# A decode kernel's last microseconds: the sum of its branches built transposed and stored from 112 partitions, one product per denominator, and the last values in three loads

## The chip, the cores and the metric

The kernel runs on one core of a Trainium2 chip. The metric is the device time of one execution in microseconds (us). Before the change it is 194.76 us (median of four runs, 194.66 to 194.98; of the first three runs, 194.69). Ratios are the mean time of one kernel's fast runs over that of the other's fast runs of the same rounds, with a 95% interval, so they are not quite the ratio of the medians quoted. "Span" is the profile's time from the first to the last instruction, some 1.8 us shorter than the device time. "Landed" is the moment at which the profile shows a transfer reported as complete. SBUF is the core's on-chip memory, which the loads fill; PSUM is where TensorE's sums build up; HBM is the chip's main memory. "Eviction" is the copy of a sum from PSUM to SBUF.

## The reference, cut to what matters

```python
# B=2 rows, D=448, 16 heads on 8 key/value heads, Dh=256, the last W=4096 of 32768 positions
xn = layernorm(x)
q  = xn @ wq
p  = softmax(q @ k_window.T * Dh**-0.5)          # k, v windows: 2*8*4096*256 bf16 each
A  = (p @ v_window) @ wo
Bo = mish(xn @ w1 + b1) @ w2
return x + A + Bo                                 # [2, 1, 448] bf16, 1792 bytes
```

77.66 MB are read for a result of 1792 bytes.

## The kernel before

All large loads go through one queue in program order (x and a bias, 5.3 KB, go through another). For each of 16 pairs of key/value head and row, K is transposed on VectorE, TensorE makes scores, ScalarE the exponentials and their sums, VectorE transposes p, TensorE multiplies with V. The last pair's values come in two loads, then wo in two.

```python
    NO = 2; DO = D // NO
    psA = [ps_a.tile([Bsz, DO], FP32, name=f"psA{n}") for n in range(NO)]
    def add(n, lhsT, rhs, **flags):
        nc.tensor.matmul(psA[n][:, :], lhsT=lhsT, rhs=rhs, skip_group_check=True, **flags)
    # ... x, then act @ w2, then per key/value head:
    def mix(kvh):                                # oT: 128 x (2 rows); w: wo, 128 x 448 per piece
        for h in range(rep):
            for n in range(NO):
                for c in range(ND):
                    add(n, oT[:, c, h, :], w[:, h, c * D + n * DO : c * D + (n + 1) * DO], ...)
    # ... per head: denominators straight from ScalarE's row sums rs
        for n in range(NH):
            nc.tensor.matmul(den[:], lhsT=rs[:, n : n + 1].to_broadcast([P, P]), rhs=hsel[:], ...)
    # ... end
    res = consts.tile([Bsz, D], BF16)            # the last tile of the constants: 896 B in each SBUF partition (row)
    nc.vector.tensor_copy(out=res[:, 0:DO], in_=psA[0][:, :])
    nc.scalar.copy(out=res[:, DO:D], in_=psA[1][:, :])
    nc.sync.dma_start(out=out.flatten_outer_dims(), in_=res[:])
```

The pools of the load tiles (wo, k, v) lie in SBUF behind the constants, in this order.

The softmax here doesn't subtract the row's maximum and nothing guards it: scores larger than these inputs give would overflow.

Of the kernel before, what the change touches and what calls it, by code (L numbers as in the profile page):

```python
# [9 lines left out]
ALU = mybir.AluOpType  # L10
AXIS = mybir.AxisListType
BF16 = mybir.dt.bfloat16
FP32 = mybir.dt.float32
# [21 lines left out]
def kernel(  # L35
# [13 lines left out]
    nc = tc.nc  # L49
    P = 128  # L50
# [3 lines left out]
    Bsz, Sq, D = A_x.shape  # L54
    _, Hkv, Sk, Dh = A_k_cache.shape
    HqDh = A_wq.shape[1]
    Hq = HqDh // Dh
    rep = Hq // Hkv
# [3 lines left out]
    T = W // P  # L62
    NH = 2
    TH = T // NH
    NX = 2
    NS = D * NX // P
    HW = HqDh // NX
    HF = F // NX
    HH = Hq // NX
    NF = HF // P  # L70
    ND = Dh // P
    NB = Dh // (2 * Q)
    NE = 2
    assert Sq == 1 and D * NX == NS * P and NS % 2 == 1 and HF % P == 0 and Hq % NX == 0
    assert TH * Q <= 512 and NB * NE * Q == Dh and ND == 2
    scale = float(Dh) ** -0.5

    consts = ctx.enter_context(tc.tile_pool(name="consts", bufs=1))
# [5 lines left out]
    small = ctx.enter_context(tc.tile_pool(name="small", bufs=3))  # L84
# [3 lines left out]
    ps_a = ctx.enter_context(tc.tile_pool(name="ps_a", bufs=1, space=PSUM))  # L88
# [3 lines left out]
    x_bf = consts.tile([Bsz, D], BF16)  # L92
# [5 lines left out]
    def v_tile(n):  # L98
        t = v_pool.tile([P, T * Dh], BF16, tag="v", name="v")
        return t[:, 0:n]  # L100
# [6 lines left out]
    for lo, hi in ((0, SC), (SC, NS)):  # L107
        w = v_tile((hi - lo) * HW).rearrange("p (s n) -> p s n", n=HW)
# [4 lines left out]
    ident = consts.tile([P, P], BF16)  # L113
# [11 lines left out]
        out=rstd[:], in_=mv[:, 1:2], func=ACT.Sqrt, bias=eps_t[:], scale=1.0  # L125
# [5 lines left out]
    for r in range(2):  # L131
        n = (NS + 1 - r) // 2
        nc.vector.tensor_scalar(  # L133
            out=xn_bf[:, r : NS : 2, :, :],
            in0=bass.AP(
                x_all.tensor,
                x_all.offset,
                [list(x_all.ap[0]), [1, n], [NS, P // 2], [(NS + r) // 2, 2]],
            ),
            scalar1=mv[:, 0:1],  # L140
            scalar2=rstd[:],
            op0=ALU.subtract,
            op1=ALU.mult,
# [3 lines left out]
    for b4 in range(NB):  # L147
        rows = slice(b4 * Q, (b4 + 1) * Q)
        for j in range(NQ):
            nc.vector.tensor_copy(  # L150
                out=spread[rows, b4, j * Q : (j + 1) * Q], in_=ident[rows, rows]
            )
    hsel = consts.tile([P, rep], FP32)
    nc.vector.tensor_copy(out=hsel[:], in_=ident[:, 0:rep])
    for j in range(1, NQ):
        nc.vector.tensor_tensor(
            out=hsel[:], in0=hsel[:], in1=ident[:, j * Q : j * Q + rep], op=ALU.add
        )
    NW = 3
    qdiag = []  # L160
    for i in range(NW):
        t = consts.tile([P, NB * NE, P], BF16, name=f"qdiag{i}")
# [5 lines left out]
    for s in range(NS):  # L168
# [7 lines left out]
        out=odd[:],  # L176
        in_=ident[:].rearrange("p (u o) -> p o u", o=2),
# [4 lines left out]
    for par in range(2):  # L182
        for x in range(NX):
            which = (par + x) % 2
            nc.vector.tensor_scalar(
                out=xs[:, par : NS : 2, x, :],
                in0=xnT_ps[:, par : NS : 2, :],
                scalar1=odd[:, which : which + 1],
                scalar2=None,
                op0=ALU.mult,  # L190
# [2 lines left out]
    nc.vector.memset(ones[:], 1.0)  # L193


    NO = 2
    DO = D // NO
    psA = [ps_a.tile([Bsz, DO], FP32, name=f"psA{n}") for n in range(NO)]

    def add(n, lhsT, rhs, **flags):  # L200
        nc.tensor.matmul(psA[n][:, :], lhsT=lhsT, rhs=rhs, skip_group_check=True, **flags)  # L201

    for n in range(NO):
        add(n, ident[0:Bsz, 0:Bsz], x_bf[:, n * DO : (n + 1) * DO], start=True, stop=False)


    qrep = consts.tile([P, NB, HH, NE, NX, Bsz], BF16)
# [28 lines left out]
    def build_q(i):  # L236
        kvh, b = heads[i]
        x, h0 = divmod(kvh * rep, HH)
        t = qdiag[i % NW]
        tv = t[:].rearrange("p (n e) c -> p n e c", e=NE)  # L240
# [9 lines left out]
    act_bf = consts.tile([P, NF, NX, Bsz], BF16)  # L250
# [53 lines left out]
    def dense_out():  # L304
        w2_sb = dense.pop("w2")
        for x in range(NX):
            for c in range(NF):
                for n in range(NO):
                    add(
                        n,  # L310
                        act_bf[:, c, x, :],
                        w2_sb[:, x, c, n * DO : (n + 1) * DO],
                        start=False,
                        stop=False,
                    )


    NSTEP = len(heads) * NH
# [3 lines left out]
    def load_k(i):  # L322
        kvh, b = heads[i]
        t = k_pool.tile([P, T * Dh], BF16, tag="k", name="k")
        nc.sync.dma_start(  # L325
            out=t[:], in_=A_k_cache[b, kvh, s0:Sk, :].rearrange("(p t) d -> p (t d)", p=P)
        )
        k_t[i] = t

    def load_v(i, parts=1):  # L330
        kvh, b = heads[i]
        t = v_tile(T * Dh).rearrange("p (t d) -> p t d", t=T)
        vin = A_v_cache[b, kvh, s0:Sk, :].rearrange("(p t) d -> p t d", p=P)
        for u in range(parts):
            ts = slice(u * T // parts, (u + 1) * T // parts)
            nc.sync.dma_start(out=t[:, ts, :], in_=vin[:, ts, :])  # L336
        v_t[i] = t

    def load_wo(kvh, parts=1):
        w = wo_pool.tile([P, rep, ND * D], BF16, tag="wo", name="wo")  # L340
        r0 = kvh * rep * Dh
        win = A_wo[r0 : r0 + rep * Dh, :].rearrange("(h p c) d -> p h (c d)", h=rep, p=P)
        for u in range(parts):
            hs = slice(u * rep // parts, (u + 1) * rep // parts)
            nc.sync.dma_start(out=w[:, hs, :], in_=win[:, hs, :])
        wo_t[kvh] = w

    def turn(s):
        kt = kt_pool.tile([P, TH * Dh], BF16, tag="kt", name="kt")
        i, half = divmod(s, NH)  # L350
        k = k_t[i] if half < NH - 1 else k_t.pop(i)
        nc.vector.transpose(  # L352
            out=kt[:].bitcast(FP32),
            in_=k[:, half * TH * Dh : (half + 1) * TH * Dh].bitcast(FP32),
        )
        kt_t[s] = kt

    def scores(s):
# [3 lines left out]
        for n in range(NB):  # L362
            for e in range(NE):
                nc.tensor.matmul(  # L364
                    psc[:],
                    lhsT=qdiag[i % NW][:, n * NE + e, :],
                    rhs=ktv[:, n, e, :, :],
# [15 lines left out]
    def turn_p(s):  # L383
        pT = p_pool.tile([P, TH * Q], BF16, tag="pT", name="pT", bufs=7)
        nc.vector.transpose(out=pT[:], in_=p_t.pop(s)[:])  # L385
        pT_t[s] = pT
        i, half = divmod(s, NH)
        if half != NH - 1:
            return
        rs = state.pop(("rs", i))  # L390
        den = ps_den.tile([P, rep], FP32, tag="den", name="den")
        for n in range(NH):
            nc.tensor.matmul(  # L393
                den[:],
                lhsT=rs[:, n : n + 1].to_broadcast([P, P]),
                rhs=hsel[:],
                start=(n == 0),
                stop=(n == NH - 1),
            )
        state["rec", i] = small.tile([P, rep], FP32, tag="rec", name="rec", bufs=4)  # L400
        nc.vector.reciprocal(out=state["rec", i][:], in_=den[:])  # L401

# [26 lines left out]
    def mix(kvh):  # L429
        oT = state["oT"]  # L430
        w = wo_t.pop(kvh)
        for h in range(rep):
            for n in range(NO):
                for c in range(ND):
                    add(
                        n,
                        oT[:, c, h, :],
                        w[:, h, c * D + n * DO : c * D + (n + 1) * DO],
                        start=False,
                        stop=(kvh == Hkv - 1 and h == rep - 1 and c == ND - 1),  # L440
                    )

    NK = len(heads)
    KA = 2
# [8 lines left out]
    for i in range(NK + KA):  # L453
        if i + 2 < NK:
            load_k(i + 2)
        if i < NK:
            load_v(i, parts=1 if i < NK - 1 else 2)
            kvh, b = heads[i]
            if b == Bsz - 1:
                load_wo(kvh, parts=1 if i < NK - 1 else 2)  # L460
            for half in range(NH):
                s = i * NH + half
                if s + 1 < NSTEP:
                    turn(s + 1)
                scores(s)
                if s >= 1:
                    turn_p(s - 1)
            if i + 2 < NK:
                build_q(i + 2)
        if i == NK:  # L470
            turn_p(NSTEP - 1)
        if i == 0:
            dense_in()
        if i == 1:
            dense_out()
        if i >= KA:
            values(i - KA)
            kvh, b = heads[i - KA]
            if b == Bsz - 1:
                mix(kvh)  # L480

    res = consts.tile([Bsz, D], BF16)
    nc.vector.tensor_copy(out=res[:, 0:DO], in_=psA[0][:, :])
    nc.scalar.copy(out=res[:, DO:D], in_=psA[1][:, :])  # L484
    nc.sync.dma_start(out=out.flatten_outer_dims(), in_=res[:])
    issue_in_order(tc)


# [28 lines left out]
```

## Time and profile before

| what | before |
|---|---|
| device time, median | 194.76 us |
| span of the profiled run | 192.7 us |
| last values landed | 187.21 us |
| store issued | 190.58 us |
| bytes loaded | 77.66 MB |

The load queue is the bound: the DMA row of the 40 slices is at nine tenths from the second slice to the 38th. What follows the last landing takes 5.5 us. The prediction below shows the lines.

```profile
SPq L512 <- DMA out_dram<-res: 0.7, 1, 0.7
```

### The profile page before, as it was taken

The page shows a single profiled execution, that of the slowest core. Times are in us where ns is not written, and L with a number is a line of the kernel's source. Part 1 is how long each engine was busy: PE and PEld are TensorE (multiplying, and loading weights), DVE is VectorE, ACT ScalarE, POOL GpSimd, SP SyncE. Part 2 cuts the span into 40 slices and gives each one's busy share as a digit, 9 for nine tenths or more (in the row PEclk, how much of TensorE's full clock was granted, in tenths as well). Part 3 has the DMA queues.
Part 4 walks back from the last instruction along what each step waited for, and adds up shares of the span by engine and source line. Part 5 has one row for each costly group of instructions (what it writes and reads, how often), then busy time and mean ns, then how long its engine had stood idle before and what let it go on. Part 6 is the DMA issues. An engine that isn't in the chain of part 4 may idle for free.

```text
span 192.7 us, 3810 instructions
## 1 busy us (share of the span) xinstructions
PE 130.4 (68%) x1624; PEld 81.3 (42%) x1624; DVE 102.2 (53%) x137; ACT 25.5 (13%) x69; POOL 24.8 (13%) x138
## 2 busy tenths in 40 slices
PE   0242993999827985499709881797449592898854
PEld 0142381466513654246504651364324452364752
DVE  4605506996638390929264753838091744748101
ACT  5000110112200211012200220021101110021100
POOL 7004320022110112002200210020200200000000
PEclk9999996699995799669975998599957979589965
DMA  6999999999999999999999999999999999999960
GB/s 211 424 447 408 427 427 435 428 435 402 431 422 428 425 415 428 435 418 414 429 425 432 420 416 430 428 425 411 428 432 428 403 434 422 432 414 429 410 253 2
DMA packets 7674, 77.90 MB, mean 404 GB/s; under 512 B 741, under 2 KB 2793, under 8 KB 3050
## 3 DMA queue, kind: packets, MB, share of 16 engines
q1 hardware_dynamic: 7652, 77.66, 96.1%
q8 instruction: 12, 0.20, 0.4%
q14 instruction: 4, 0.03, 0.0%
q10 hardware_dynamic: 6, 0.01, 0.0%
HBM read 77.67 MB, written 0.00 MB: 403 GB/s over the span
## 4 chain that ended last, share of the span: by engine, by line
DMA 96%; PE 1%; SPq 1%; issue 0%; ACT 0%; DVE 0%
DMA v<-in_A_v_cache_dram 51%; DMA k<-in_A_k_cache_dram 18%; DMA wo<-in_A_wo_dram 17%; DMA v<-in_B_w_dram 10%; PE psA L201 1%; PE o L411 1%; SPq L109 0%; SPq L325 0%; ACT res L484 0%; DVE oT L422 0%; SPq L336 0%
## 5 line engine op out<-in xcount | busy, mean ns | idle before, releaser
L352 DVE STREAM_TRANSPOSE kt<-k 128x2048 f32<-128x2048 f32 x32 | 73.5, 2300 | 48.9 <-DMA k<-in_A_k_cache_dram 48.9
L364 PE MATMUL sc<-kt,qdiag 128*128 128x512 bf16 x256 | 75.0, 443 | 14.4 <-DVE kt L352 14.3
L364 PEld LDWEIGHTS <-qdiag 128*128 128x128 bf16 x256 | 26.1, 111 | 50.5 <-issue 24.1
L374 ACT ACTIVATE p<-sc 128x512 bf16<-128x512 f32 x32 | 19.1, 597 | 144.8 <-PE sc L364 140.9
L244 POOL COPY qdiag<-qrep 32x8 bf16<-32x8 bf16 x128 | 21.0, 186 | 125.3 <-PE sc L364 109.8
L201 PE MATMUL psA<-wo,oT 128*2 128x224 bf16 x64 | 12.5, 370 | 31.3 <-DVE oT L422 31.3
L411 PEld LDWEIGHTS <-v 128*128 128x128 bf16 x1024 | 27.9, 97 | 6.3 <-DMA v<-in_A_v_cache_dram 3.0
L411 PE MATMUL o<-pT,v 128*128 128x2 bf16 x1024 | 28.1, 163 | 2.7 <-DMA v<-in_A_v_cache_dram 2.7
L385 DVE STREAM_TRANSPOSE pT<-p 128x512 bf16<-128x512 bf16 x32 | 21.4, 671 | 0.0
L201 PEld LDWEIGHTS <-oT 128*2 128x2 bf16 x64 | 6.5, 111 | 34.6 <-DVE oT L422 32.0
L393 PEld LDWEIGHTS den<-hsel,rs 128*128 128x128 f32 x64 | 11.7, 227 | 3.8 <-issue 2.1
L401 DVE RECIPROCAL rec<-den 128x2 f32<-128x2 f32 x16 | 2.5, 153 | 18.7 <-PE den L393 18.7
L393 PE MATMUL den<-hsel,rs 128*128 128x2 f32 x64 | 9.4, 252 | 0.0
L215 PE MATMUL qT_ps<-xs,v 128*128 128x4 bf16 x112 | 3.3, 166 | 6.1 <-DMA v<-in_A_wq_dram 6.1
L422 DVE TENSOR_TENSOR oT<-o,rec 128x4 bf16<-128x4 f32 x16 | 2.1, 134 | 8.5 <-PE o L411 8.5
L374 ACT ACTIVATION_READ_ACCUMULATOR p<-sc 128x1 f32 x32 | 6.2, 194 | 0.0
L215 PEld LDWEIGHTS <-v 128*128 128x128 bf16 x112 | 3.1, 104 | 6.6 <-DMA v<-in_A_wq_dram 6.6
L224 DVE CAST qT<-qT_ps 128x64 bf16<-128x64 f32 x1 | 0.2, 225 | 7.0 <-PE qT_ps L215 7.0
L169 PE MATMUL xnT_ps<-ident,xn_bf 2*128 2x2 bf16 x7 | 0.5, 166 | 5.0 <-DVE xn_bf L133 5.0
L270 PE MATMUL hT_ps<-xs,v 128*128 128x4 bf16 x49 | 3.7, 195 | 0.0
L270 PEld LDWEIGHTS <-v 128*128 128x128 bf16 x49 | 3.2, 149 | 0.3
L201 PE MATMUL psA<-v,act_bf 128*2 128x224 bf16 x28 | 2.8, 259 | 0.0
(40 smaller groups left out, 22.5 us busy)
## 6 DMA issues: line engine op xcount, KB each, us to landing
k<-in_A_k_cache_dram SPq DMA_DIRECT2D x16, 2048.0 KB, 32.5
v<-in_A_v_cache_dram SPq DMA_DIRECT2D x15, 2048.0 KB, 34.8
v<-in_B_w_dram SPq DMA_DIRECT2D x2, 1568.0 KB, 21.2
wo<-in_A_wo_dram SPq DMA_DIRECT2D x7, 448.0 KB, 31.8
v<-in_A_wq_dram SPq DMA_DIRECT2D x1, 2048.0 KB, 7.8
v<-in_A_v_cache_dram SPq DMA_DIRECT2D x2, 1024.0 KB, 29.9
v<-in_A_wq_dram SPq DMA_DIRECT2D x1, 1536.0 KB, 11.1
wo<-in_A_wo_dram SPq DMA_DIRECT2D x2, 224.0 KB, 24.1
```

Source lines behind the costliest of these rows:

```text
L201: nc.tensor.matmul(psA[n][:, :], lhsT=lhsT, rhs=rhs, skip_group_check=True, **flags)
L215: nc.tensor.matmul(qT_ps[:, hh, e, :], lhsT=wq_v[s][:, hh, e, :], rhs=xs[:, s, :, :].rearrange("p x b -> p (x b)"), start=(s == 0), stop=( ...
L244: nc.gpsimd.tensor_copy(out=tv[rows, :, e, j * Q : j * Q + rep], in_=qrep[rows, :, h0 : h0 + rep, e, x, b],)
L270: nc.tensor.matmul(hT_ps[:, c, :, :].rearrange("p x b -> p (x b)"), lhsT=w1_v[:, s, c, :], rhs=xs[:, s, :, :].rearrange("p x b -> p (x b)" ...
L352: nc.vector.transpose(out=kt[:].bitcast(FP32), in_=k[:, half * TH * Dh : (half + 1) * TH * Dh].bitcast(FP32),)
L364: nc.tensor.matmul(psc[:], lhsT=qdiag[i % NW][:, n * NE + e, :], rhs=ktv[:, n, e, :, :], start=(n == 0 and e == 0), stop=(n == NB - 1 and ...
L374: nc.scalar.activation(out=p_sb[:], in_=psc[:].rearrange("p t c -> p (t c)"), func=ACT.Exp, scale=scale, accum_out=state["rs", i][:, s % N ...
L385: nc.vector.transpose(out=pT[:], in_=p_t.pop(s)[:])
L393: nc.tensor.matmul(den[:], lhsT=rs[:, n : n + 1].to_broadcast([P, P]), rhs=hsel[:], start=(n == 0), stop=(n == NH - 1),)
L401: nc.vector.reciprocal(out=state["rec", i][:], in_=den[:])
L411: nc.tensor.matmul(po[:, c, :], lhsT=vv[:, t, c, :], rhs=pTv[:, th, 0:rep], start=(t == 0 and c == 0), stop=(t == T - 1), skip_group_check ...
L422: nc.vector.tensor_tensor(out=oT[:, :, :, b], in0=po[:], in1=state.pop(("rec", i))[:].unsqueeze(1).to_broadcast([P, ND, rep]), op=ALU.mult,)
```

## The change

Its intent is a shorter tail: half as many products after the last landing, one cheap eviction of eight columns instead of two of 224, and half the FP32 products. The core of the diff:

```diff
-    psA = [ps_a.tile([Bsz, DO], FP32, name=f"psA{n}") for n in range(NO)]
+    NO = 4; DO = D // NO                                    # 112
+    psA = ps_a.tile([DO, NO, Bsz], FP32, name="psA")
+    def add(w, rhs, start=False, stop=False):
+        for c in range(NO):
+            nc.tensor.matmul(psA[:, c, :], lhsT=w[:, c : D : NO], rhs=rhs, ...)
 ...
-            load_v(i, parts=1 if i < NK - 1 else 2)
+            load_v(i, (0, T) if i < NK - 1 else (0, T // 2, 3 * T // 4, T))
 ...
-        for n in range(NH):
-            nc.tensor.matmul(den[:], lhsT=rs[:, n:n+1].to_broadcast([P, P]), rhs=hsel[:], ...)
+        # sums = hsel * rs[:, 0:1], then sums += hsel * rs[:, 1:2], on VectorE
+        nc.tensor.matmul(den[:], lhsT=ones_f[:], rhs=sums[:], start=True, stop=True)
 ...
-    res = consts.tile([Bsz, D], BF16)
+    res = consts.tile([DO, Bsz, NO], BF16)                  # 16 B a partition
+    nc.vector.tensor_copy(out=res[:].rearrange("p b c -> p c b"), in_=psA[:])
+    nc.sync.dma_start(
+        out=out.flatten_outer_dims().rearrange("b (p c) -> p b c", c=NO), in_=res[:])
```

The store now has 112 x 2 runs of 8 bytes.

More of the change, by code (lines that the diff above doesn't have):

```diff
@@ L73 @@
     NE = 2
-    assert Sq == 1 and D * NX == NS * P and NS % 2 == 1 and HF % P == 0 and Hq % NX == 0
+    assert Sq == 1 and D % 4 == 0 and D * NX == NS * P and NS % 2 == 1 and HF % P == 0 and Hq % NX == 0
     assert TH * Q <= 512 and NB * NE * Q == Dh and ND == 2
@@ L158 @@
         )
+    ones_f = consts.tile([P, P], FP32)
+    nc.gpsimd.memset(ones_f[:], 1.0)
     NW = 3
@@ L193 @@
     nc.vector.memset(ones[:], 1.0)
-    NO = 2
+    NO = 4
     DO = D // NO
-    psA = [ps_a.tile([Bsz, DO], FP32, name=f"psA{n}") for n in range(NO)]
-    def add(n, lhsT, rhs, **flags):
-        nc.tensor.matmul(psA[n][:, :], lhsT=lhsT, rhs=rhs, skip_group_check=True, **flags)
-    for n in range(NO):
-        add(n, ident[0:Bsz, 0:Bsz], x_bf[:, n * DO : (n + 1) * DO], start=True, stop=False)
+    psA = ps_a.tile([DO, NO, Bsz], FP32, name="psA")
+    def add(w, rhs, start=False, stop=False):
+        for c in range(NO):
+            nc.tensor.matmul(
+                psA[:, c, :],
+                lhsT=w[:, c : D : NO],
+                rhs=rhs,
+                start=start and c == 0,
+                stop=stop,
+                skip_group_check=True,
+            )
+    add(x_bf[:, :], ident[0:Bsz, 0:Bsz], start=True)
     qrep = consts.tile([P, NB, HH, NE, NX, Bsz], BF16)
@@ L307, in dense_out @@
             for c in range(NF):
-                for n in range(NO):
-                    add(
-                        n,
-                        act_bf[:, c, x, :],
-                        w2_sb[:, x, c, n * DO : (n + 1) * DO],
-                        start=False,
-                        stop=False,
-                    )
+                add(w2_sb[:, x, c, :], act_bf[:, c, x, :])
     NSTEP = len(heads) * NH
@@ L328, in load_k, with load_v @@
         k_t[i] = t
-    def load_v(i, parts=1):
+    def load_v(i, cuts=(0, T)):
         kvh, b = heads[i]
@@ L333, in load_v @@
         vin = A_v_cache[b, kvh, s0:Sk, :].rearrange("(p t) d -> p t d", p=P)
-        for u in range(parts):
-            ts = slice(u * T // parts, (u + 1) * T // parts)
-            nc.sync.dma_start(out=t[:, ts, :], in_=vin[:, ts, :])
+        for lo, hi in zip(cuts, cuts[1:]):
+            nc.sync.dma_start(out=t[:, lo:hi, :], in_=vin[:, lo:hi, :])
         v_t[i] = t
@@ L390, in turn_p @@
         rs = state.pop(("rs", i))
-        den = ps_den.tile([P, rep], FP32, tag="den", name="den")
-        for n in range(NH):
-            nc.tensor.matmul(
-                den[:],
-                lhsT=rs[:, n : n + 1].to_broadcast([P, P]),
-                rhs=hsel[:],
-                start=(n == 0),
-                stop=(n == NH - 1),
-            )
+        sums = small.tile([P, rep], FP32, tag="sums", name="sums")
+        nc.vector.tensor_scalar(
+            out=sums[:], in0=hsel[:], scalar1=rs[:, 0:1], scalar2=None, op0=ALU.mult
+        )
+        nc.vector.scalar_tensor_tensor(
+            out=sums[:], in0=hsel[:], scalar=rs[:, 1:2], in1=sums[:], op0=ALU.mult, op1=ALU.add
+        )
+        den = ps_den.tile([P, rep], FP32, tag="den", name="den")
+        nc.tensor.matmul(den[:], lhsT=ones_f[:], rhs=sums[:], start=True, stop=True)
         state["rec", i] = small.tile([P, rep], FP32, tag="rec", name="rec", bufs=4)
@@ L432, in mix @@
         for h in range(rep):
-            for n in range(NO):
-                for c in range(ND):
-                    add(
-                        n,
-                        oT[:, c, h, :],
-                        w[:, h, c * D + n * DO : c * D + (n + 1) * DO],
-                        start=False,
-                        stop=(kvh == Hkv - 1 and h == rep - 1 and c == ND - 1),
-                    )
+            for c in range(ND):
+                add(
+                    w[:, h, c * D : (c + 1) * D],
+                    oT[:, c, h, :],
+                    stop=(kvh == Hkv - 1 and h == rep - 1 and c == ND - 1),
+                )
     NK = len(heads)
@@ L480 @@
                 mix(kvh)
-    res = consts.tile([Bsz, D], BF16)
-    nc.vector.tensor_copy(out=res[:, 0:DO], in_=psA[0][:, :])
-    nc.scalar.copy(out=res[:, DO:D], in_=psA[1][:, :])
-    nc.sync.dma_start(out=out.flatten_outer_dims(), in_=res[:])
+    res = consts.tile([DO, Bsz, NO], BF16)
+    nc.vector.tensor_copy(out=res[:].rearrange("p b c -> p c b"), in_=psA[:])
+    nc.sync.dma_start(
+        out=out.flatten_outer_dims().rearrange("b (p c) -> p b c", c=NO), in_=res[:]
+    )
     issue_in_order(tc)
```

## The prediction

> **What bounds the kernel now.** I read the page's chain of work that ended last, then the same chain in order of time, then the windows and the timeline of the last 12 us.
>
> The chain of the page, by engine, and the rows of the 40 slices:
>
> ```profile
> DMA 96%; PE 1%; SPq 1%; issue 0%; ACT 0%; DVE 0%
> ...
> DMA  6999999999999999999999999999999999999960
> GB/s 211 424 447 408 427 427 435 428 435 402 431 422 428 425 415 428 435 418 414 429 425 432 420 416 430 428 425 411 428 432 428 403 434 422 432 414 429 410 253 2
> ```
>
> The reader is to see that the loads run without a hole from the second slice to the 38th at some 425 GB/s. 77.66 MB have to come in, and no compute engine holds them up. Only what follows the last load can be shortened by a change that moves the same bytes.
>
> The end of the chain in order of time (start in us, duration in us, what):
>
> ```profile
> 156.59 30.62 DMA v<-in_A_v_cache_dram
> 187.21 0.05 issue
> 187.26 1.02 PE o L411 x32
> 188.28 0.02 issue
> 188.31 0.18 DVE oT L422
> 188.48 0.04 issue
> 188.53 1.67 PE psA L201 x8
> 190.19 0.02 issue
> 190.22 0.34 ACT res L484
> ```
>
> So 187.21 us is the last piece of values landing. After it come 32 products of the second half of the last head, the normalisation, eight products with wo, the eviction and the store. The timeline has the store and its neighbours (start, duration, instruction):
>
> ```profile
> 189.84 0.38 DVE L483 CAST res<-psA 2x224 bf16<-2x224 f32 x1 [1.37 <-PE psA L201]
> 190.22 0.34 ACT L484 CAST res<-psA 2x224 bf16<-2x224 f32 x1 [11.00 <-PE psA L201]
> 190.58 0.34 SPq L485 DMA_DIRECT2D out_dram<-res  x1
> ```
>
> From the store's issue at 190.58 to the span's end at 192.7 are 2.1 us. The device time (194.53 us in the profiled run) is 1.8 us more than the span, which I hold constant. The tail that the change can touch is therefore 192.7 - 187.2 = 5.5 us, or 2.8% of the time.
>
> TensorE's clock in that tail, from the windows (the number after the busy times is the granted clock, then DMA share and GB/s):
>
> ```profile
> 188.00:189.00 1.00, 0.74 (x14) 0.52 (x11) 0.17 (x1) 0.00 (x0) 0.00 (x0) 0.50 0.00 0
> 189.00:190.00 1.00, 1.00 (x7) 0.50 (x4) 0.16 (x1) 0.00 (x0) 0.00 (x0) 0.50 0.00 0
> ```
>
> The array runs at half clock there.
>
> **What the Trainium skill says.** (1) "TensorE: Matmul & The Clock Gate", Part 1: the clock is gated to half after an idle window and the ratio is binary. The trace agrees: 0.50 above, and the wo products follow each other at (1.67 - 0.39) / 7 = 183 ns (0.39 is the longest of them in the tile's view), about 224 columns at 1.2 GHz. (2) Same page, "Weight-path perf modes": fast weight load is on when the number of weights is 128 and the type is not FP32. The trace fits: 128-column weights of v go by in (1.02 - 0.16) / 31 = 28 ns in the half-clock tail. It also has a slow case: the w1 products (128 columns, read with a step of 7 elements) take (0.53 - 0.16) / 6 = 61 ns each at full clock, against (1.75 - 0.16) / 63 = 25 ns for v (step 2). (3) "VectorE: DVE Perf Modes", the TRN2 errata: a PSUM source costs 120 + FD cycles at 0.96 GHz, 358 ns for 224 elements; measured 380. (4) "DMA: Bandwidth & Descriptors", Specifications: transfers under 512 B are written by read-modify-write. The store before has two runs of 896 B, so this trace cannot show it.
>
> **The change part by part.**
>
> Last values in three loads (1/2, 1/4, 1/4). The two last pieces now land one after the other. The first half landed at about 184.7 and the second at 187.2, 2.5 us for 1 MB, so the third quarter should land near 186.0 and the last again at 187.2. After it 16 products remain, not 32: 15 x 0.028 + 0.16 = 0.58 in place of 1.02. That is **-0.44 us**, on the path. The quarter before needs 0.58 and has 1.2, so it is done. The load adds one DMA of the same bytes: nothing.
>
> Sum built transposed. In the last mix, 8 products with 2 weight columns and 224 moving columns become 16 with 112 weight columns (step 4 elements) and 2 moving columns. 112 is not 128 and the step is larger than v's, so I choose the slow weight load. From w1's 61 ns at full clock: 61 x 112/128 = 53 ns, and twice that, 107 ns, at half clock; 112 columns at 1.2 GHz would be 93. With 15 x 0.093..0.107 + 0.16 the mix takes 1.56 to 1.77 us against 1.67: **about 0**, say -0.02. This is the term I trust least: with the fast load it would be 15 x 0.028 + 0.16 = 0.58, or -1.1 us. The seven earlier mixes (16 products each) and the 56 products of w2 (before 28 of 259 ns) lie beside the loads and cost nothing.
>
> Eviction. Two casts of 2x224 (380 on VectorE, overlapped; 335 ns on ScalarE, on the path) become one VectorE cast of 112x8. By form of the cast: 380 ns less (224 - 8) / 0.96 = 155 ns; the oT product (128x4 from PSUM, 134 to 171 ns) says the same. **-0.18 us.**
>
> Store. 2 runs of 896 B become 112 x 2 = 224 runs of 8 B. The wo loads have 256 runs and their issue takes 0.33 to 0.38 us against 0.34, so issue is equal. If 16 DMA engines share the 112 partitions, each writes 14 runs instead of a single one. In the packet records each of the two 896 B packets of the store takes 45 ns and a 4 B semaphore write 9 ns; with 20 to 50 ns a run, 14 make 0.3 to 0.7 us. I take **+0.3 us**, an estimate, since no 8 B write is in this trace.
>
> One product per denominator. Per head, two FP32 products (two passes each; 4 weight loads, 0.61 us in the tail) become one (about 0.35), and two 128x2 vector instructions of about 0.15 us come ahead of it. VectorE's total rises by 16 x 0.3 = 5 us on 102, off the path. But the product now waits for VectorE: before, it needed only the row sums from ScalarE, and now sums queue behind the transpose of p. Before, the denominator of head 14 was at 175.56 on TensorE and its transpose on VectorE at 176.45. Now it comes after 176.45 + 0.67 + 0.3 = 177.4, and the last scores move from 176.58 to about 177.8, **1.2 us later on TensorE**. Followed on at full clock: scores to 179.7, values of head 13 to 181.5, mix to 182.6, transpose and sums on VectorE to 182.7, denominator to 183.15, values of head 14 (landed 182.25) to 184.85, first half of the last values to 185.7, third quarter (after 186.0) to 186.5. The last piece lands at 187.2, so 0.7 us of slack stay: **0 on the path**.
>
> Setup: one more memset on GpSimd ahead of qdiag, not needed before 16.7 us: 0.
>
> Sum: -0.44 - 0.02 - 0.18 + 0.3 = **-0.34 us**, 194.69 to 194.35.
>
> **Rivals.**
> (a) The last mix waits for wo. wo's two parts are queued behind the values; issued at 161.55 and 166.38, with 26.2 and 21.9 us to landing, they land at 187.8 and 188.3. The mix would start at 188.09 with part one and need part two after eight products, at 188.09 + 8 x 0.1 = 188.9. With the fast load it would need it at 188.3: at most 0.1 us lost. Unlikely to show at the rate I assume.
> (b) Fast weight load holds for 112 columns with step 4: 193.3 us. For it: v's step 2 is fast too. Against: the 128-column condition and w1's 61 ns. I give it 15%.
> (c) The 8 B store costs over 1 us: 195.0 us or more. For it: read-modify-write, and neighbouring runs written by different DMA engines into one line. Against: 14 runs per DMA engine are few. 15%.
> (d) TensorE becomes late at the end, because the denominator waits for VectorE and the clock is at half during the last scores (3.6 instead of 1.9 us, as at 166.2). That eats the 0.7 us and leaves up to 1 us: 195.3 us. The clock windows in this trace were full from 170.5 to 184.1. 10%.
> (e) Loads are held up in the middle because buffers come free later. The trace's queue waits almost only for earlier landings and has some 30 us from issue to landing, so a delay of 1 us in freeing cannot reach it. 2%.
>
> **Range and chances.** The three runs before lie within 0.17 us. Around 194.35, (b) pulls down by 1.1 and (c), (d) up by up to 1. Range **193.6 to 195.0 us**. Faster by over 2% (below 190.8) would need 3.9 of the 5.5 us of tail, which no sum of parts gives: 1%. Slower by over 2% (above 198.6) needs a broken load stream or a store of 4 us: 2%. Within 2%: 97%.
>
> **What would show it.** Right: DMA still at over 90% in all slices to 187 us and the last values landing within 0.3 us of 187.2; 16 products in about 0.58 us after it; the last mix as 16 pairs at 93 to 107 ns with the clock at 0.50; one cast of about 155 ns; a store of 224 packets of 8 B taking a few tenths longer. The denominator should wait for VectorE in all heads with no effect on landings. Wrong: a mix of 0.6 us (fast load), a gap between mix parts that ends with wo, the last values' products starting later than their landing, or a store that takes over 1 us more.

## The result, and the profile after

The changed kernel takes 195.53 us (four runs, 195.34 to 195.77) against 194.76: ratio 1.0039, interval 1.0021 to 1.0056. It is slower by a little, outside the predicted range of 193.6 to 195.0.

The end of its chain of waits in order of time (start, us, what), to be held against the same lines of before:

```profile
160.29 25.72 DMA v<-in_A_v_cache_dram
186.01 0.05 issue
186.06 0.60 PE o L412 x16
186.66 0.02 issue
186.68 0.18 DVE oT L423
186.86 0.04 issue
186.90 1.74 PE psA L204 x16
188.64 0.02 issue
188.67 0.17 DVE res L481
```

The reader is to see two things. The last values land at 186.01, where they landed at 187.21 before: 1.20 us earlier, though the same bytes are moved. And from that landing to the eviction's end all goes as the change intended: 0.60 in place of 1.02, one cast of 0.17. Yet the span is 193.9 us, not 192.7. What is left is the store. From the timeline, its issue; from the list of DMA issues, its size and the us from issue to landing; from the queue's own waits (what waits, for what: us in total, times, longest), the wait for it at the program's end:

```profile
188.86 0.35 SPq L482 DMA_DIRECT2D out_dram<-res  x1
```

```profile
out_dram<-res SPq DMA_DIRECT2D x1, 1.8 KB, 4.0
```

```profile
SPq L511 <- DMA out_dram<-res: 3.6, 1, 3.6
```

The wait for the store is 3.6 us where it was 0.7. The windows show that the DMA engines do nothing in most of it (start and end in us, busy times of the five engines, granted clock, DMA share, GB/s):

```profile
189.00:190.00 1.00, 0.00 (x0) 0.00 (x0) 0.00 (x0) 0.00 (x0) 0.00 (x0) 0.50 0.13 2
190.00:191.00 1.00, 0.00 (x0) 0.00 (x0) 0.00 (x0) 0.00 (x0) 0.00 (x0) 0.50 0.00 0
191.00:192.00 1.00, 0.00 (x0) 0.00 (x0) 0.00 (x0) 0.00 (x0) 0.00 (x0) 0.50 0.00 0
```

The packet records agree: 224 packets of 8 B start at 189.72, take 9 ns each, and the last ends at 189.95. The landing is told at 192.86, 2.9 us later. The Trainium skill says where such time goes: "DMA: Bandwidth & Descriptors", "Anatomy of one DMA", puts most of a DMA's fixed cost into the write receipt, because the semaphore cannot fire before the last byte is confirmed landed. The page says it of transfers issued from GpSimd; this store was issued from SyncE. The changed kernel's trace agrees on the place, and gives the size: 2.9 us of the 4.0 from issue to landing. The kernel before does not: its 896 B runs ended at 191.42 and the queue's wait at 191.75, 0.33 us of 1.17.

The balance of the two profiled runs, each stretch from the lines above:

| stretch | before | after | difference |
|---|---|---|---|
| start to last values landed | 187.21 | 186.01 | -1.20 |
| landing to store issued | 3.37 | 2.85 | -0.52 |
| store issued to end of span | 2.14 | 5.05 | +2.91 |
| span | 192.72 | 193.91 | +1.19 |

(The profiled runs differ by 1.24 us of device time, the medians by 0.77.) The last row but one is the loss. The first row is a gain that nobody asked for. Both need experiments.

### The profile page after: what moved, and what is told of

The parts are those of the page before. It is cut to its first block, busy times and chain, and to the rows that moved or that the text cites. A ratio compares the mean times of both kernels' runs of the same rounds, so it can differ in the third digit from the quotient of the medians.

```text
span 193.9 us, 3939 instructions
## 1 busy us (share of the span) xinstructions
PE 134.6 (69%) x1686; PEld 87.8 (45%) x1686; DVE 108.6 (56%) x169; ACT 25.1 (13%) x68; POOL 25.3 (13%) x139
## 4 chain that ended last, share of the span: by engine, by line
DMA 87%; PE 6%; DVE 3%; issue 0%; SPq 0%
DMA k<-in_A_k_cache_dram 70%; DMA v<-in_A_v_cache_dram 13%; DMA v<-in_A_wq_dram 4%; PE sc L365 3%; DVE kt L353 2%; PE psA L204 2%; PE o L412 1%; DVE pT L386 1%; DVE oT L423 0%; SPq L337 0%; PE den L400 0%; DVE res L481 0%; SPq L327 0%
## 5 line engine op out<-in xcount | busy, mean ns | idle before, releaser
L365 PE MATMUL sc<-kt,qdiag 128*128 128x512 bf16 x256 | 79.2, 463 | 7.5 <-DVE kt L353 7.5
L365 PEld LDWEIGHTS <-qdiag 128*128 128x128 bf16 x256 | 28.5, 120 | 42.8 <-issue 24.8
L412 PEld LDWEIGHTS <-v 128*128 128x128 bf16 x1024 | 28.2, 97 | 4.3 <-DMA v<-in_A_v_cache_dram 0.9
L204 PE MATMUL psA<-oT,wo 128*112 128x2 bf16 x128 | 13.8, 238 | 20.8 <-DVE oT L423 20.8
L204 PEld LDWEIGHTS <-wo 128*112 128x112 bf16 x128 | 14.5, 198 | 20.6 <-issue 20.4
L400 PEld LDWEIGHTS den<-sums,ones_f 128*128 128x128 f32 x32 | 7.2, 246 | 20.7 <-DVE sums L396 18.1
L400 PE MATMUL den<-sums,ones_f 128*128 128x2 f32 x32 | 6.2, 264 | 13.8 <-DVE sums L396 13.8
L204 PEld LDWEIGHTS <-v 128*112 128x112 bf16 x56 | 6.0, 201 | 0.5 <-issue 0.5
L204 PE MATMUL psA<-act_bf,v 128*112 128x2 bf16 x56 | 5.9, 242 | 0.0
L224 PEld LDWEIGHTS <-v 128*128 128x128 bf16 x112 | 3.2, 104 | 6.0 <-DMA v<-in_A_wq_dram 6.0
L396 DVE SCALAR_TENSOR_TENSOR sums<-hsel,rs,sums 128x2 f32<-128x2 f32 x16 | 3.5, 221 | 0.6
```

The lines of the kernel that those rows point to most:

```text
L204: nc.tensor.matmul(psA[:, c, :], lhsT=w[:, c : D : NO], rhs=rhs, start=start and c == 0, stop=stop, skip_group_check=True,)
L224: nc.tensor.matmul(qT_ps[:, hh, e, :], lhsT=wq_v[s][:, hh, e, :], rhs=xs[:, s, :, :].rearrange("p x b -> p (x b)"), start=(s == 0), stop=( ...
L365: nc.tensor.matmul(psc[:], lhsT=qdiag[i % NW][:, n * NE + e, :], rhs=ktv[:, n, e, :, :], start=(n == 0 and e == 0), stop=(n == NB - 1 and ...
L396: nc.vector.scalar_tensor_tensor(out=sums[:], in0=hsel[:], scalar=rs[:, 1:2], in1=sums[:], op0=ALU.mult, op1=ALU.add)
L400: nc.tensor.matmul(den[:], lhsT=ones_f[:], rhs=sums[:], start=True, stop=True)
L412: nc.tensor.matmul(po[:, c, :], lhsT=vv[:, t, c, :], rhs=pTv[:, th, 0:rep], start=(t == 0 and c == 0), stop=(t == T - 1), skip_group_check ...
```

## The experiments

**First set: the parts alone.** Five rounds each. Theory S: the store alone costs the time. Rival D: the denominator's new wait, or the extra load, holds things up.

*e1_rows_sum*: the changed kernel with before's sum and store.

```diff
 # the changed kernel
-    psA = ps_a.tile([DO, NO, Bsz], FP32, name="psA")        # and its add, mix, eviction, store
+    psA = [ps_a.tile([Bsz, DO], FP32, name=f"psA{n}") for n in range(NO)]   # all as before
```

> The changed kernel with the sum of before (two rows, wo as the moving operand, store of two runs of 896 B); one product per denominator and three loads stay. Theory S (the store of 224 runs of 8 B takes 4.0 us from issue to landing against about 1.2, and that alone costs the time): 0.44 us under before by the shorter last values, so 194.3 us; if the loads also end 1.2 us earlier because of these two parts, 193.1. Rival D (the denominator's wait for VectorE, or the extra load, holds things up): stays at 195.2 or more.

Measured: 194.63 us, ratio to before 0.9992 (0.9979 to 1.0004). Rival D falls: without the store the loss is gone. But the gain is 0.16 us, not 0.44.

*e2_transposed_only*: before with the transposed sum and its store alone.

```diff
 # the kernel before
-    psA = [ps_a.tile([Bsz, DO], FP32, name=f"psA{n}") for n in range(NO)]
+    psA = ps_a.tile([DO, NO, Bsz], FP32, name="psA")        # and its add, mix, eviction, store
```

> The kernel before with the transposed sum and its store alone. Theory S: +2.85 us for the store, +0.07 for the mix, -0.17 for the eviction, so 2.7 us over before, 197.5 us; 196.2 if the earlier end of the loads seen in the changed kernel (1.2 us) belongs to this part. Rival D: within 0.3 us of before.

Measured: 195.53 us, ratio 1.0041 (1.0027 to 1.0055). This part makes the whole of the difference. The store's wait is 3.4 us, but the last values landed at 185.53, 1.7 us earlier than before. So the early landing belongs to this part too (the end of its chain, as above):

```profile
155.27 30.26 DMA v<-in_A_v_cache_dram
185.53 0.05 issue
```

*e3_loads_only* and *e4_den_only*:

```diff
 # e3: the kernel before
-            load_v(i, parts=1 if i < NK - 1 else 2)
+            load_v(i, (0, T) if i < NK - 1 else (0, T // 2, 3 * T // 4, T))
```

```diff
 # e4: the kernel before
-        for n in range(NH): nc.tensor.matmul(den[:], lhsT=rs[:, n:n+1].to_broadcast([P, P]), rhs=hsel[:], ...)
+        # sums on VectorE
+        nc.tensor.matmul(den[:], lhsT=ones_f[:], rhs=sums[:], start=True, stop=True)
```

> The kernel before with the last values in three loads alone. Theory S: 16 products after the last landing in place of 32, -0.44 us, 194.3 us. If the loads end 1.2 us earlier because of the cut: 193.1 us. Rival D: no gain or a loss, 194.8 us or more.

> The kernel before with one product per denominator alone. Theory S: hidden behind the loads, 194.8 us; TensorE's last denominators some 1 us later, last values still started by their landing. If it makes the loads end earlier: 193.6. Rival D: slower by 0.5 us or more.

Measured: e3 194.48 us, ratio 0.9990 (0.9977 to 1.0002); e4 194.73 us, 0.9999 (0.9986 to 1.0011). The last values landed at 187.65 and 187.34. In e3 the 16 products took 0.60 us as planned, and its profiled landing was 0.44 us later than before's, so a single profile cannot show a gain of that size; the interval of the timed runs includes -0.2% and zero. The other pairs of runs that differ only in the third load put its gain at 0.30 us (e8 against e5) and 0.16 us (e9 against e10). The single product is neutral. In e1, where both are in, the profile shows TensorE late: it went through the last 128 products without a pause (start, us, instruction):

```profile
184.71 3.54 PE L412 MATMUL o<-pT,v 128*128 128x2 bf16 x128
```

They ended at 188.25. The last values had landed at 187.46, so 16 products could have been done at about 187.50 + 0.60 = 188.10. The wait for VectorE cost at most 0.15 us there.

**Second set: why the loads end earlier.** The transposed sum makes the last constant tile smaller (16 B a partition, rounded to 32, in place of 896), and all load tiles lie behind it. In the compiled programs (addresses in bytes within a partition; "modulo" is the rest after division) the first k tile starts at 43360 before, at 43360 - 864 = 42496 in e2, and at 43360 - 864 + 512 (the 128 FP32 ones) = 43008 in the changed kernel. The other load tiles have the same remainder modulo 512. Theory A: the start of the tiles that the loads write sets the rate. Rival M: wo as the fixed operand, or chance.

The edit of these runs is one number, the result tile's length; the instructions stay (e7 lengthens the transposed result tile from 16 to 64 B; e8 and e9 have the three loads as well). The tiles that the engines work on lie behind the load tiles and move too, so the packet records below, which are of the loads alone, have to decide:

```diff
-    res = consts.tile([Bsz, D], BF16)
+    res = consts.tile([Bsz, D + 16], BF16)   # 32 B more; 32 elements are 64 B, 80 are 160 B, 208 are 416 B
```

> The kernel before with its last constant tile 32 B longer, so that all tiles of loads behind it start at a multiple of 64 B (k at 43392 instead of 43360); same instructions, same bytes. Theory A (in the kernels with the transposed sum the loads end some 1.5 us earlier because the smaller result tile moved the load tiles from 32 to 0 modulo 64): last values land at about 185.6 us instead of 187.2, time 193.2 us. Rival M (the earlier end comes from wo being the fixed operand, or is chance): no change, 194.7 us.

> Control: the same tile 64 B longer, so the load tiles move but stay at 32 modulo 64. Theory A: as before, 194.8 us, last values at 187.2. If any shift of the addresses changes the time by more than 0.5 us, theory A in this form falls.

> The changed kernel with its result tile 32 B longer, load tiles back at 32 modulo 64. Theory A: the loads end 1.5 us later, 195.5 + 1.5 = 197.0 us, the full cost of the store shows. Rival M: 195.5 us, last values landed at 186.0 as in the changed kernel.

> The kernel before with the last values in three loads and the 32 B of padding: no transposed sum, no new store. Theory A with S: -0.3 for the loads as measured and -1.5 for the start of the tiles, 193.0 us, faster than both kernels. Rival M: 194.5 us.

Measured: e5 194.73 us, 0.9993 (0.9980 to 1.0007); e6 194.66 us, 0.9993 (0.9980 to 1.0005); e7 197.77 us, 1.0155 (1.0139 to 1.0170); e8 194.43 us, 0.9980 (0.9967 to 0.9992). Theory A was wrong in its form: a start at a multiple of 64 or 128 B gives nothing (e5, e8). But e7 speaks against rival M: the changed kernel's own instructions, with load tiles moved by 32 B, lose 2.2 us. Its last values landed at 188.04:

```profile
162.18 25.86 DMA v<-in_A_v_cache_dram
188.04 0.05 issue
```

So the boundary had to be larger. Both early kernels had starts at multiples of 512 B.

> The kernel before with the last values in three loads and 160 B of padding, so the load tiles start at 0 modulo 512 (k at 43520), as in the changed kernel and the run with the transposed sum alone. 32 B of padding (0 modulo 128, 384 modulo 512) gave nothing. Theory A512 (only a start at a multiple of 512 B, or 256, makes the loads end earlier): last values at about 186.0, 192.9 us, faster than both kernels. Rival M (the gain needs the transposed sum's instructions as well): 194.4 us.

> The kernel before with the 160 B alone. Theory A512: packets of wo take 74 ns and those of 16 KiB 611 ns almost without exception, last values at about 185.7 instead of 187.2, 193.2 us. Rival M: 194.7 us, packets scattered as before (90th percentile 82 and 620 ns).

> The kernel before with 416 B: load tiles at 256 modulo 512, 0 modulo 256. If the boundary is 256 B: 193.2 us as with 160 B. If it is 512 B: 194.7 us. Rival M: 194.7 us.

Measured: e10 192.92 us, ratio 0.9917 (0.9902 to 0.9931); e11 192.85 us, 0.9913 (0.9898 to 0.9927); e9 192.76 us, 0.9900 (0.9884 to 0.9917). The kernel before, with nothing changed but the length of one tile, is 1.6 us faster. The end of e10's chain beside that of before in the prediction (start, us, what):

```profile
155.07 30.40 DMA v<-in_A_v_cache_dram
185.47 0.05 issue
185.52 1.03 PE o L411 x32
186.55 0.02 issue
186.57 0.18 DVE oT L422
186.75 0.04 issue
186.79 1.67 PE psA L201 x8
188.46 0.02 issue
188.48 0.34 ACT res L484
```

Everything after the landing is as it was; the landing is 1.74 us earlier. e11 fixes the boundary: 256 B past a multiple of 512 is as good as a multiple of 512, 128 B past a multiple of 256 (e5, e8) is not. Over all kernels:

| start of load tiles modulo 256 | kernels | last values landed (us) |
|---|---|---|
| 0 | changed, e2, e9, e10, e11, s1 to s4 | 185.46 to 186.01 |
| 32 | e7 | 188.04 |
| 96 | before, e1, e3, e4 | 187.21 to 187.65 |
| 128 | e5, e8 | 187.40 to 187.64 |
| 160 | e6 | 187.32 |

The packet records show it load by load (ns that a packet took; 90th percentile in brackets):

| packet | before | e5 (128) | e10 (0) | e11 (0) |
|---|---|---|---|---|
| 1792 B (wo and parts of it, 2048 packets) | 76.4 (82) | 76.7 (82) | 74.4 (74) | 74.5 (74) |
| 16 KiB (4096 packets) | 619.7 (620) | 619.1 (619) | 615.4 (611) | 615.5 (611) |

With starts at multiples of 256 B nearly all packets of a size take the same time; otherwise they scatter upward. Per DMA engine 4096 / 16 = 256 packets of 16 KiB lose (619.7 - 615.4) x 256 = 1.1 us, and 128 of 1792 B lose 2.0 x 128 = 0.26 us. That is 1.4 of the 1.7 us. In e7 (32 B past a multiple) the means are 620.8 and 76.9 ns, in the changed kernel 615.6 and 74.0: by the same sum 1.3 and 0.4 us, 1.7 of the 2.0 us between their landings.

With the boundary known, e2 and e10 weigh the store in timed runs. In both the load tiles start at a multiple of 256 B, and they differ only in the transposed sum with its store: 195.53 against 192.92 us, 2.6 us more (not run in the same rounds), though mix and eviction together are 0.1 us shorter there.

The Trainium skill has the boundary. "DMA: Bandwidth & Descriptors", "How a descriptor splits into AXI transactions": a transaction "must start from a 256B-aligned address", and one that does not start there needs an extra piece. The page says it of reads, and here the side that moved is what the loads write. The boundary agrees; the cost does not follow from the page's pieces. An estimate by its way of counting them in beats of 32 B, for a start 96 B past the boundary: 59 in place of 56 for 1792 B, 5%, and 515 in place of 512 for 16 KiB, 0.6%; measured were 2.7% and 0.7%. For e7's 32 B the estimate is smaller, 0.2% for 16 KiB, and the measured cost is larger, 0.9%. Why 32 B past the boundary costs more than 96 is open.

**Third set: the store's cost by itself.** Theory L: small writes into one block of memory wait for each other. Theory N: each write under 512 B costs, wherever it goes. The base is e9's kernel (its fast store kept); behind its store comes a second store of a constant tile to a scratch tensor in HBM, and nothing else changes.

```diff
 # e9's kernel, the padding cut by the 32 B that the constant tile takes
+    dum = consts.tile([112, 2, 4], BF16)                    # set to zero early
+    scr = nc.dram_tensor("scratch", [112, 2, 256], BF16).ap()   # s1: one run per 512 B; s4: [112, 2, 32], per 64 B
+    nc.sync.dma_start(out=scr[:, :, 0:4], in_=dum[:])
 # s2: scr is [2, 448], written dense as the output of the changed kernel
```

```diff
 # s3: the changed kernel, contiguous columns of wo, so that the store has 896 runs of 2 B
-                lhsT=w[:, c : D : NO],
+                lhsT=w[:, c * DO : (c + 1) * DO],
-        out=out.flatten_outer_dims().rearrange("b (p c) -> p b c", c=NO), in_=res[:]
+        out=out.flatten_outer_dims().rearrange("b (c p) -> p b c", c=NO), in_=res[:]
```

> The store's cost by itself: rows sum and fast store, load tiles at 0 modulo 512, and behind the store a second one of 224 runs of 8 B from 112 partitions to a scratch tensor in HBM, each run in a block of 512 B of its own (result unchanged). Theory L (writes of 8 B into the same block of memory wait for each other): about 1.2 us from issue to landing. Theory N (every write under 512 B costs, whatever its neighbours): 4.0 us as in the changed kernel.

> Control for the scratch store with 512 B blocks: the same second store of 224 runs of 8 B, now dense in 1792 B as the output is. Theory L (writes into one block wait for each other): about 2.9 us from its last packet to its landing as in the changed kernel, against 0.43 us with blocks of 512 B; span some 2.5 us longer. Theory N (number of writes alone): 0.43 us again, and then the changed kernel's cost would lie elsewhere.

> The scratch store with one 8 B run per 64 B. If writes hold each other up within 64 B only: 0.4 us from last packet to landing, as with 512 B. If the block is 512 B (8 runs each): between 0.4 and 2.9 us. If the block is larger or the number counts: 2.9 us.

> The changed kernel with contiguous columns of wo per product, so that the store has 896 runs of 2 B in place of 224 of 8 B (same 1792 B, same 112 partitions, result right). Theory L with one write after the other per block: four times 2.9, about 11.6 us from last packet to landing, time about 204 us. If only the number of blocks counts: 2.9 us again, 195.5 us.

One execution each. The queue's waits for the store at the end, s1:

```profile
SPq L515 <- DMA scratch<-dum: 1.3, 1, 1.3
```

s2:

```profile
SPq L515 <- DMA scratch<-dum: 2.8, 1, 2.8
```

s3:

```profile
SPq L511 <- DMA out_dram<-res: 12.4, 1, 12.4
```

| run | runs of the store | span (us) | last packet to landing or to the end of the wait (us) |
|---|---|---|---|
| s1 | 224 of 8 B, each in 512 B of its own | 192.6 | 191.13 to 191.56: 0.43 |
| s4 | 224 of 8 B, each in 64 B of its own | 192.4 | 190.88 to 191.31: 0.43 |
| s2 | 224 of 8 B, dense | 193.8 | 190.72 to 192.70: 1.98 |
| changed | 224 of 8 B, dense | 193.9 | 189.95 to 192.86: 2.91 |
| s3 | 896 of 2 B, dense | 202.1 | 189.82 to 201.03: 11.21 |

Theory N falls: 224 writes of 8 B cost 0.43 us when each has 64 B to itself. Theory L holds in this much: the cost is there only when the runs lie densely (s1 and s4 against s2), and it grows with the number of runs for the same 1792 B, 2.91 us / 224 = 13.0 ns and 11.21 / 896 = 12.5 ns each (s3 makes the runs shorter as well as more). e2 and e7, with the changed kernel's store, repeat its number: 2.85 and 2.79 us from last packet to landing.

That the waiting is inside blocks of 64 B is not shown: s2 differs from s4 also in lying within 1792 B in place of 14 KB. In the trace the store's landing is reported in 16 steps. In s1 they come within 0.16 us; in the changed kernel they are spread from 191.21 to 192.86, and in s3 even the first comes 9.0 us after the last packet. That fits writes of all DMA engines waiting for each other better than each engine working through its own 14 runs.

My number for s2 was a miss: 1.98 us, not 2.9, and its span is 1.2 us longer than s1's, not 2.5. What makes the same dense store cheaper on a scratch tensor behind another store is open, and so is why the waiting runs through all 224 and not only through the eight of one 64 B block.

## Why the prediction was wrong, point by point

It said 194.35 us and a range up to 195.0; measured were 195.53.

- **The step that failed first: the store**, "with 20 to 50 ns a run, 14 make 0.3 to 0.7 us. I take +0.3 us". Measured +2.9 us (2.91 in the balance). The packets themselves were cheaper than I assumed, 9 ns. The term was worked out per DMA engine, 14 runs in parallel with 15 other engines, and had no wait after the last packet; in the changed kernel and in s3 that wait is 13 ns for every run of the whole store, as if the runs went one after the other (s2's 1.98 us would be 8.8 ns, so 13 is no constant). Rival (c), neighbouring runs of different DMA engines in one line, was given 15%. Dense runs are indeed what costs; the line and the part of different engines stay unproven. Its counter-argument, "14 runs per DMA engine are few", was the error, and the prediction's own sign, "a store that takes over 1 us more", came.
- **A term that was missing**: "a change that moves the same bytes" was held to be unable to touch the loads, and the last values were put at 187.2. They landed at 186.01. A result tile shorter by 864 B had moved the load tiles to multiples of 256 B; in the kernel before that alone is worth 1.6 us by the timed runs (e10). It hid over half of the store's cost, by chance and not by design: moved 32 B off the boundary, the changed kernel takes 197.77 (e7). The reading that the loads leave nothing to gain before the last landing was wrong in another way too. The windows of the kernel before show the DMA engines less than half busy in the last microsecond of it (columns as above):

```profile
186.00:186.50 0.50, 0.00 (x0) 0.00 (x0) 0.00 (x0) 0.00 (x0) 0.00 (x0) 0.50 0.42 168
186.50:187.00 0.50, 0.00 (x0) 0.00 (x0) 0.00 (x0) 0.00 (x0) 0.00 (x0) 0.50 0.18 61
```

  Three of the 16 steps in which that load's landing is reported come at 187.13 to 187.21, the other 13 by 185.89. What an even share between the engines would save was not tried.
- **Last values in three loads**, -0.44: the 16 products took 0.60 us, as worked out, and the quarter before was done in time. In the time it shows as -0.1% with an interval that includes zero (e3).
- **The mix**, about 0: 1.74 against 1.67 us. The fast weight load did not come, rival (b) fell. The result was right and the working was not: I took 61 ns at full clock, scaled it to 112 columns and doubled it for the half clock. In the changed kernel the pairs follow each other by 104 ns at full and at half clock alike, so that 104 lies in my 93 to 107 is luck; with contiguous columns (s3) by 52 and 93 ns. Half clock scales the contiguous load and not the one with a step of 4.
- **Eviction**, -0.18: a cast of 0.17 in place of 0.34, and from the mix's end to the store's issue 0.22 in place of 0.39. Right.
- **One product per denominator**, 0: right in the time (e4). Its two vector instructions took 0.19 and 0.22 us, not 0.15. The denominator of head 14 did wait for VectorE. Rival (d), TensorE late at the end, was seen once, in e1, for about 0.15 us. In the changed kernel TensorE had been idle for 0.64 us when the last values landed, against the 0.7 of slack worked out:

```profile
186.06 0.59 PE L412 MATMUL o<-pT,v 128*128 128x2 bf16 x16 [0.64 <-DMA v<-in_A_v_cache_dram]
```

- **Rivals (a) and (e)**: no gap in the mix ended with wo, and no hole came into the loads. Both fell.

Sum of the measured parts: -1.6 (e10) - 0.2 (e3) - 0.1 (mix and eviction) + 2.9 (store) = +1.0 us, against +0.77 measured.

The experiments point to a better kernel than both: before, with the last values in three loads and load tiles at a multiple of 256 B (e9), 192.76 us, 1.0% under before and 2.8 us under the changed kernel.

## What to carry to other kernels

Count a scattered store by all its runs that lie beside each other in memory, not by the share of one DMA engine (here some 13 ns a run), and look from its last packet to its landing: the DMA share read zero there. Where a kernel is bound by its loads, look at where their tiles start in SBUF; a tile of any length placed ahead of them can move them on or off a multiple of 256 B, which was worth 1.6 us here. A change to a small tile is therefore also a change to all addresses behind it, and an experiment that undoes one part has to keep these addresses fixed.

## What the Trainium skill lacked or had wrong

- "DMA: Bandwidth & Descriptors", Specifications and the section on small descriptors: says that transfers under 512 B are slow; lacks that it depends on the neighbours. 224 writes of 8 B ended 0.43 us after their last packet with 64 B or 512 B each, and 2.0 to 2.9 us after it when dense; 896 dense writes of 2 B took 11.2 us.
- Same page, "How a descriptor splits into AXI transactions": gives the 256 B boundary for the start of reads, and a cost in beats that the measured one does not follow; it has nothing on where a load's writes start. Here the start of the load's tile in SBUF gave 76.4 against 74.4 ns for 1792 B and 619.7 against 615.4 ns for 16 KiB (96 B past the boundary and on it), 0.8% of the kernel's time.
- "TensorE: Matmul & The Clock Gate", LDWEIGHTS: gives a time by the number of columns alone. With 112 columns the pairs followed each other by 52 ns (full clock) and 93 ns (half) for contiguous columns, and by 104 ns at both clocks with a step of 4 elements.
